# Pooled keys and values: one strided reduction in place of three additions

## Chip, core and metric

The kernel runs on one core of one Trainium2 chip. What is measured is the time of one execution in device microseconds (us). The engines of the core are named as in the profile: PE (TensorE matmuls), PEld (its weight loads), DVE (VectorE), ACT (ScalarE), POOL (GpSimd) and SP (SyncE, which issues most transfers).

## What is computed

Attention over keys and values that are averaged in groups of eight rows, then two feed-forward layers. Batch 8, 8 heads, 576 rows, head size 64; 4608 tokens of width 512, inner width 2048; float32.

```python
def _attn_ref(q, k, v):
    pool, Sp, scale = 8, S // 8, 1.0 / np.sqrt(D)
    k_p = k.reshape(B, H, Sp, pool, D).mean(axis=3)
    v_p = v.reshape(B, H, Sp, pool, D).mean(axis=3)
    scores = scale * np.matmul(q, k_p.transpose(0, 1, 3, 2))
    scores = scores - np.max(scores, axis=-1, keepdims=True)
    attn = np.exp(scores)
    attn = attn / (np.sum(attn, axis=-1, keepdims=True) + 1e-09)
    return np.matmul(attn, v_p)

x = attn_out.transpose(0, 2, 1, 3).reshape(B * S, H * D)
h = x @ moe_w_in;  x = np.maximum(0.01 * h, h) @ moe_w_out
h = x @ moe2_w_in; r = np.maximum(h, 0.0); out = (r * r) @ moe2_w_out
```

## The kernel before

Attention goes batch by batch (8), each in chunks of at most 128 query rows (five per batch). For each batch the pooled keys and values are prepared first. A head has 72 pooled rows: 64 of them lie in large tiles of 128 partitions (two heads, one above the other; two such pairs per tile), the last 8 of all heads together in one small tile of 64 partitions. The transfers of `load_main` (L354) and `load_rest` (L368) put the eight rows that belong together side by side in one partition, 8 x 64 = 512 words, so a large tile is 128 x 2 x 512 and a small one 64 x 1 x 512.

`pooled` (L340) sums the eight rows on DVE. It halves the width three times: 512 to 256 to 128 to 64 words per pooled row. The first two steps write into the tile itself, the last into the destination; each step reads what the one before wrote. For a large tile the steps are 512, 256 and 128 columns wide, for a small one 256, 128 and 64. The factor 1/8 is applied later by ACT.

`prepare_k` (L398) calls `pooled` for the small tile and for two large ones, then PE transposes the sums (L412, L415) and ACT writes the key matrix `kT`. `prepare_v` (L431) does the same for values: POOL multiplies the small sum by a mask (L437), transfers copy the product (L445), ACT and DVE split the large sums into a high and a low part (L459, L460). A batch thus has six sums, and there are eight batches.

Beside attention the first layer starts at once, on the tokens that are ready. Its weights are decoded on ACT and DVE (`decode`, L181: passes over 128 x 1024 words at L187 to L198, then L208; the inputs `low` and `high` take every second word of the staged tile) and split into two parts on ACT and DVE (L226, L227, and L807, L808 for the inner activations), because each product is made by three matmuls (L301). The staged weights come through a ring of two tiles.

The first batch is in an order written out by hand (`first_batch`, L621, held by `in_order`, L89: on each engine the instructions keep the order of the program). Behind it a planner orders the instructions of every engine, on the whole along the program's order, where steps of attention are dealt out between the units of the first layer (`advance`, L1077; rates at L60). Attention is done some 490 us into the span; later come the preparation of the second layer's weights and the block products of both layers.

Of the kernel before, what the change touches and what calls it, by code (L numbers as in the profile page):

```python
# [12 lines left out]
ALU = mybir.AluOpType  # L13
AX = mybir.AxisListType
# [4 lines left out]
POOL = 8  # L19
# [14 lines left out]
def attention_two_mlps(  # L34
# [11 lines left out]
    nc = tc.nc  # L46
    B, H, S, D = q.shape
# [261 lines left out]
    def attention():  # L309

        with ExitStack() as s:
# [10 lines left out]
                out=mask, in_=mask, compare_op=ALU.is_ge, fill=0.0, base=0,  # L322
# [3 lines left out]
                out=mask, in_=mask, compare_op=ALU.is_ge, fill=0.0, base=KR - 1,  # L326
# [12 lines left out]

            def pooled(dst, src):  # L340

                for n in (POOL * D // 2, POOL * D // 4, D):
                    nc.vector.tensor_tensor(
                        out=dst if n == D else src[:, :, 0:n], in0=src[:, :, 0:n], in1=src[:, :, n:2 * n], op=ALU.add
                    )

            def kv_tile(b, rows, n, name):

# [49 lines left out]
            def prepare_k(b):  # L398
                kr, kk = KV.pop(("k", b))
                i = b % 2  # L400
                kd = ap1.tile([P, NP, D], F32, tag="kd", name=f"kd{b}")
                rr = ap1.tile([KR * H, 2, D], F32, tag="rr", name=f"rr{b}")
                pooled(rr[:, 0:1], kr)
                nc.vector.tensor_copy(rr[:, 1], rr[:, 0])
                for m in range(0, NP, 2):
                    pooled(kd[:, m:m + 2], kk[m // 2])
                    yield
# [23 lines left out]
            def prepare_v(b):  # L431
                vr, vv = KV.pop(("v", b))
                vd = ap1.tile([P, NP, D], F32, tag="vd", name=f"vd{b}")
                rd = ap1.tile([KR * H, 1, D], F32, tag="rd", name=f"rd{b}")
                pooled(rd, vr)
                rv = ap1.tile([KR * H, H, D], F32, tag="rv", name=f"rv{b}")
                nc.gpsimd.tensor_tensor(  # L437
# [35 lines left out]
            for b in range(B):  # L473
                at = 0
                for span in range(len(SPANS)):
                    off = 0
                    while off < SPANS[span]:
                        n = min(P, SPANS[span] - off)
# [704 lines left out]
```

## Time and profile before

| | us |
|---|---|
| median of 3 runs | 1657.63 (1656.99 to 1659.5) |
| profiled run | 1661.4 |
| span of the profiled execution | 1659.6 |
| DVE busy in the span | 1277.1 (77%) |
| PE busy in the span | 1609.5 (97%) |
| POOL busy in the span | 130.2 (8%) |
| L343 busy on DVE, 0 to 400 us | 69.3 |

The profile is one execution; the span is from its first to its last instruction, and the run's time holds 1.8 us more. Busy shares over the whole span mix stages with different limits, so they are read stretch by stretch. The chain of work that ended last is followed back from the last instruction.

### The profile page before, as it was taken

The numbers are of one execution on the slowest core, as the hardware profiler recorded it, in microseconds if no ns is written. First come the engines' busy times: TensorE is split into PE (matmuls) and PEld (weight loads), VectorE is DVE, ScalarE is ACT, GpSimd is POOL, SyncE is SP. The second block draws the span as 40 slices with busy tenths as digits, with TensorE's granted clock in tenths as the row PEclk, the third lists the DMA queues.
The fourth block names the chain that finished last, engine by engine and source line by source line (L and its number), as shares of the span: only waits on it lengthen the run. The fifth ranks groups of instructions, "written<-read, shape, count | busy, mean of one in ns | idle before, by whom it ended". The sixth has DMA issues, their size and how long they took to land.

```text
span 1659.6 us, 27187 instructions
## 1 busy us (share of the span) xinstructions
PE 1609.5 (97%) x9976; PEld 1514.8 (91%) x9976; DVE 1277.1 (77%) x1893; ACT 895.5 (54%) x1602; POOL 130.2 (8%) x149
## 2 busy tenths in 40 slices
PE   5889999999999999999999999999999999999998
PEld 4667778888888999999999999999999999999998
DVE  5999899878678988979989569378477486485474
ACT  5768655655667867667677425334234234244233
POOL 3131323223210000000000000000000000000000
PEclk8999999999999999999999999999999999999999
DMA  7666565867435778888897777878878878878775
GB/s 180 174 206 186 163 176 161 246 194 206 127 101 198 263 272 280 270 301 277 281 317 251 254 261 270 301 255 289 288 252 296 283 251 302 273 253 272 265 251 190
DMA packets 223716, 399.74 MB, mean 241 GB/s; under 512 B 56160, under 2 KB 129888, under 8 KB 223584
## 3 DMA queue, kind: packets, MB, share of 16 engines
q1 hardware_dynamic: 223264, 397.48, 72.6%
q8 instruction: 80, 1.31, 0.3%
q10 hardware_dynamic: 320, 0.52, 0.1%
q14 instruction: 52, 0.43, 0.1%
HBM read 318.77 MB, written 77.59 MB: 239 GB/s over the span
## 4 chain that ended last, share of the span: by engine, by line
PE 81%; DVE 10%; DMA 3%; ACT 3%; issue 2%; SPq 0%; POOL 0%; ACTq 0%; DVEq 0%; POOLq 0%
PE h L304 13%; PE h L306 13%; PE h L305 13%; PE acc L306 12%; PE acc L304 12%; PE acc L305 12%; PE s L513 1%; DVE gl L808 1%; DVE wm L198 1%; ACT x L530 1%; DMA wb_in<-ws_in 1%; PE pt L563 1%; DMA st_in_out<-in_moe_w_out_dram 1%; PE trq L492 1%; DVE ol L868 1%
## 5 line engine op out<-in xcount | busy, mean ns | idle before, releaser
L867 ACT CAST oh<-g 128x768 fp32r<-128x768 f32 x252 | 210.2, 835 | 261.9 <-PE acc L305 163.6
L304 PE MATMUL h<-xh,wb_in 128*128 128x384 f32 x1008 | 338.0, 335 | 5.5 <-ACT s L970 3.9
L306 PE MATMUL h<-xh,wb_in 128*128 128x384 f32 x1008 | 337.5, 335 | 0.0
L305 PE MATMUL h<-xl,wb_in 128*128 128x384 f32 x1008 | 337.4, 335 | 0.0
L868 DVE TENSOR_TENSOR ol<-g,oh 128x768 fp32r<-128x768 f32 x252 | 240.3, 953 | 81.2 <-ACT oh L867 80.8
L306 PE MATMUL acc<-wb_out,ol 128*128 128x256 f32 x1008 | 282.2, 280 | 0.0
L304 PE MATMUL acc<-wb_out,oh 128*128 128x256 f32 x1008 | 281.2, 279 | 0.0
L305 PE MATMUL acc<-wb_out,oh 128*128 128x256 f32 x1008 | 281.2, 279 | 0.0
L304 PEld LDWEIGHTS h<-xh,wb_in 128*128 128x128 f32 x1008 | 189.8, 188 | 7.4 <-ACT s L970 4.5
L306 PEld LDWEIGHTS h<-xh,wb_in 128*128 128x128 f32 x1008 | 189.7, 188 | 0.0
L305 PEld LDWEIGHTS h<-xl,wb_in 128*128 128x128 f32 x1008 | 189.7, 188 | 0.0
L305 PEld LDWEIGHTS acc<-wb_out,oh 128*128 128x128 f32 x1008 | 189.5, 188 | 0.0
L306 PEld LDWEIGHTS acc<-wb_out,ol 128*128 128x128 f32 x1008 | 189.2, 188 | 0.0
L304 PEld LDWEIGHTS acc<-wb_out,oh 128*128 128x128 f32 x1008 | 188.5, 187 | 0.0
L871 DVE TENSOR_TENSOR g<-g,g 128x768 f32<-128x768 f32 x144 | 135.8, 952 | 1.1
L304 PE MATMUL h<-xh,hl_in 128*128 128x512 f32 (+1 forms) x320 | 124.1, 388 | 11.4 <-ACT hl_in L226 6.0
L976 DVE TENSOR_TENSOR g<-h,s 128x768 f32<-128x768 f32 x36 | 34.4, 956 | 125.6 <-issue 75.2
L304 PE MATMUL acc<-gh,hl_out 128*128 128x512 f32 (+1 forms) x320 | 120.0, 383 | 1.2 <-ACT hl_out L226 1.1
L306 PE MATMUL h<-xh,hl_in 128*128 128x512 f32 (+1 forms) x320 | 120.8, 377 | 0.1
L305 PE MATMUL h<-xl,hl_in 128*128 128x512 f32 (+1 forms) x320 | 120.3, 376 | 0.0
L944 DVE SCALAR_TENSOR_TENSOR g<-g 128x768 f32<-128x768 f32 x96 | 91.2, 954 | 37.3 <-ACT g L993 36.4
L305 PE MATMUL acc<-gl,hl_out 128*128 128x512 f32 (+1 forms) x320 | 118.5, 373 | 0.9 <-DVE gl L808 0.9
(149 smaller groups left out, 3138.0 us busy)
## 6 DMA issues: line engine op xcount, KB each, us to landing
wb_in<-wd_in SPq DMA_DIRECT2D x204, 512.0 KB, 4.2
wb_out<-wd_out SPq DMA_DIRECT2D x204, 512.0 KB, 4.4
xs<-x SPq DMA_DIRECT2D x18, 768.0 KB, 6.2
wb_in<-ws_in SPq DMA_DIRECT2D x48, 256.0 KB, 4.3
wb_out<-ws_out SPq DMA_DIRECT2D x48, 256.0 KB, 3.3
out_dram<-o SPq DMA_DIRECT2D x24, 384.0 KB, 5.1
q<-in_q_dram SPq DMA_DIRECT2D x32, 256.0 KB, 3.8
v<-in_v_dram SPq DMA_DIRECT2D x64, 128.0 KB, 3.7
```

The lines of the kernel that those rows point to most:

```text
L198: nc.vector.scalar_tensor_tensor(out=m, in0=high, scalar=0xC0000000, in1=m, op0=ALU.bitwise_and, op1=ALU.bitwise_or)
L304: nc.tensor.matmul(outp, ah, bh, start=first, stop=False, **kw)
L305: nc.tensor.matmul(outp, ah, bl, start=False, stop=False, **kw)
L306: nc.tensor.matmul(outp, al, bh, start=False, stop=last, **kw)
L492: nc.tensor.transpose(tr[:, m, :n], t[:n, 2 * m:2 * m + 2].rearrange("p a d -> p (a d)"), ident[:n, :n])
L513: nc.tensor.matmul(sc[:n, 2 * m:2 * m + 2].rearrange("p a x -> p (a x)"), qT[:, 2 * e + m, :n], kT[b % 2][:, 2 * e + m].rearrange("p a x - ...
L530: nc.scalar.activation(x[:n, 4 * e + h], sc[:n, h], AF.Exp, bias=mx[:n, h], accum_out=sm[:n, 4 * e + h],)
L867: nc.scalar.copy(hi, src)
L868: nc.vector.tensor_tensor(out=lo, in0=src, in1=raw(hi), op=ALU.subtract)
L871: nc.vector.tensor_tensor(out=out_, in0=a, in1=b, op=ALU.subtract)
L944: nc.vector.scalar_tensor_tensor(out=g, in0=g, scalar=0.0, in1=g, op0=ALU.max, op1=ALU.mult)
L976: nc.vector.tensor_tensor(out=g11, in0=v, in1=s1, op=ALU.add)
```

## The change

Only `pooled` changes. The three additions become one reduction. Its input is a view of the same tile in which, for each pooled row m and each column d, the eight values j stand innermost; since a row of 64 words lies between two of them, neighbouring elements of the view are 64 words apart. The tile is no longer written. Every call, its place in the program and its destination stay.

```diff
             def pooled(dst, src):
 
-                for n in (POOL * D // 2, POOL * D // 4, D):
-                    nc.vector.tensor_tensor(
-                        out=dst if n == D else src[:, :, 0:n], in0=src[:, :, 0:n], in1=src[:, :, n:2 * n], op=ALU.add
-                    )
+                nc.vector.tensor_reduce(
+                    out=dst, in_=src.rearrange("p m (j d) -> p m d j", j=POOL), axis=AX.X, op=ALU.add
+                )
```

## Rows read from the trace of the kernel before

**Rows 1.** The page: the chain that ended last, shares of the span by engine.
```profile
PE 81%; DVE 10%; DMA 3%; ACT 3%; issue 2%; SPq 0%; POOL 0%; ACTq 0%; DVEq 0%; POOLq 0%
```

**Rows 2.** By stretch: us; PE, PEld, DVE, ACT, POOL busy (instructions); clock; DMA share, GB/s.
```profile
0.00:40.00 40.00, 21.96 (x104) 18.40 (x105) 23.56 (x56) 23.29 (x106) 16.48 (x30) 0.89 0.75 182
40.00:200.00 160.00, 141.91 (x663) 110.85 (x662) 148.90 (x261) 117.58 (x315) 40.53 (x32) 0.95 0.62 183
200.00:320.00 120.00, 116.99 (x622) 96.76 (x621) 109.53 (x239) 69.70 (x160) 29.90 (x34) 1.00 0.63 187
320.00:400.00 80.00, 80.00 (x438) 67.45 (x437) 65.12 (x133) 44.08 (x93) 21.62 (x25) 1.00 0.71 206
```

**Rows 3.** The same stretches, line L343 alone: us, busy (instructions), clock, DMA.
```profile
0.00:40.00 40.00, 7.37 (x18) 0.89 0.75 182
40.00:200.00 160.00, 24.06 (x54) 0.95 0.62 183
200.00:320.00 120.00, 22.80 (x45) 1.00 0.63 187
320.00:400.00 80.00, 15.05 (x27) 1.00 0.71 206
400.00:1659.60 1259.60, 0.00 (x0) 1.00 0.75 257
```

**Rows 4.** DVE in order of time, 56 to 67 us: start, duration, instruction.
```profile
57.39 0.69 DVE L343 TENSOR_TENSOR k<-k 128x512 f32<-128x512 f32 x1
...
60.41 1.22 DVE L198 SCALAR_TENSOR_TENSOR wm<-st_in_out,wm 128x1024 uint32<-128x1024 uint32 x1
61.55 0.68 DVE L227 TENSOR_TENSOR hl_out<-w,hl_out 128x512 fp32r<-128x512 f32 x1
...
64.42 0.42 DVE L343 TENSOR_TENSOR k<-k 128x256 f32<-128x256 f32 x1
64.76 0.68 DVE L227 TENSOR_TENSOR hl_in<-w,hl_in 128x512 fp32r<-128x512 f32 x1
65.36 0.69 DVE L191 TENSOR_SCALAR wm<-wm 128x1024 f32<-128x1024 f32 x1
...
65.96 0.29 DVE L343 TENSOR_TENSOR kd<-k 128x128 f32<-128x128 f32 x1
66.16 0.69 DVE L194 TENSOR_SCALAR wm<-wm 128x1024 uint32<-128x1024 uint32 x1
```

**Rows 5.** DVE's groups by form: count | busy us, mean ns | idle before.
```profile
L343 DVE TENSOR_TENSOR v<-v 128x512 f32<-128x512 f32 x16 | 14.1, 880 | 0.9 <-DMA v<-in_v_dram 0.9
L343 DVE TENSOR_TENSOR vd<-v 128x128 f32<-128x128 f32 x16 | 9.0, 571 | 0.1
```

**Rows 6.** POOL and DVE in order of time at 82 us.
```profile
82.03 1.74 POOL L437 TENSOR_TENSOR rv<-rd,mask 64x512 f32<-64x512 f32 x1
...
82.54 1.38 DVE L343 TENSOR_TENSOR vd<-v 128x128 f32<-128x128 f32 x1
```

**Rows 7.** DVE's reductions and L198 by form; POOL's product in order of time.
```profile
L523 DVE TENSOR_REDUCE mx<-s 128x4 f32<-128x288 f32 x64 | 27.5, 453 | 7.7 <-PE s L513 6.9
L198 DVE SCALAR_TENSOR_TENSOR wm<-st_in_out,wm 128x1024 uint32<-128x1024 uint32 x16 | 19.6, 1226 | 0.1
L540 DVE TENSOR_REDUCE sm<-x 128x8 f32<-128x576 f32 x20 | 15.0, 749 | 3.2 <-ACT x L539 3.1
...
18.68 1.04 POOL L545 TENSOR_TENSOR p<-x,rs 128x512 f32<-128x512 f32 x1 [3.39 <-DVE rs L543]
```

**Rows 8.** All engines in order of time, first batch, 7 to 29 us.
```profile
7.84 1.15 DVE L343 TENSOR_TENSOR k<-k 128x512 f32<-128x512 f32 x2 [1.76 <-DMA k<-in_k_dram]
...
10.76 0.47 PE L412 MATMUL trk<-ident,kd 128*128 128x128 f32 x1 [0.85 <-DVE kd L343]
...
26.23 1.15 DVE L343 TENSOR_TENSOR v<-v 128x512 f32<-128x512 f32 x2
...
28.18 1.04 POOL L545 TENSOR_TENSOR p<-x,rs 64x512 f32<-64x512 f32 x1 [5.52 <-ACT qT L496]
```

## The prediction, made before the result

> **What bounds the kernel now.** I read the page first: TensorE (PE) carries 81% of the chain that ended last, VectorE (DVE) 10% of it [rows 1]. A whole-span average hides the stage, so I then cut the span into stretches [rows 2]. From 400 us on, the changed code is gone: line L343 has no instruction there [rows 3], and from 320 us to 400 us PE has no idle time at all. What is changed can only act before 320 us. In 0 to 40 us PE is busy 22.0 of 40 us: this is the hand-ordered first batch. In 40 to 200 us PE is busy 141.9 of 160 us, so it loses 18.1 us, and DVE is busy 148.9 us, so DVE has only 11.1 us left: there DVE is the tightest engine. In 200 to 320 us PE loses 3.0 us of 120. After 320 us PE is full, so the change is worth what it does to PE's start on that full stretch: at most PE's idle time ahead of it can be won, and any time by which DVE delays PE there is lost for good.
>
> **What the change removes.** Six sums are made per batch (for keys and for values: one of 64 partitions, two of 128), eight batches, 48 sums. Each is three additions now, 144 instructions, and becomes one reduction, 48. The trees occupy DVE 7.4 us in 0 to 40 us (18 instructions, four large and two small sums), 24.1 us in 40 to 200 us (54: twelve large, six small), 22.8 us in 200 to 320 us (45: ten large, five small) [rows 3]. The 15.1 us after 320 us lie beside a full PE and are priced at nothing; without that cover they would count as those of the stretch before.
>
> How long a tree really holds DVE is seen in the start times, since neighbours overlap: behind an addition of 512 columns the next instruction starts 0.60 us later, behind 256 columns 0.34, behind 128 columns 0.20 us, and behind a pass over 1024 columns 1.14 us [rows 4]. So a large tree that is not disturbed costs 0.60 + 0.34 + 0.20 = 1.14 us, although its three durations add to 1.4 us: the removal of two instructions is worth far less than their durations. The tree reads 896 pairs, the reduction reads 1024 single elements; the tree pays three starts, the reduction one. At equal speed per element they draw.
>
> What the trees do lose is time beside GpSimd (POOL): the rows of values stand at a mean of 880 ns for 512 columns and 571 ns for 128 [rows 5], against 0.69 and 0.29 us where POOL is idle [rows 4]. One case: an addition of 128 columns takes 1.38 us while POOL's product with the mask takes 1.74 us [rows 6]. That is why 24.1 us stand in 40 to 200 us where twelve large sums at 1.14 us and six small ones at about 0.67 (0.34 + 0.20 + some 0.13 us for 64 columns, an estimate) would make 17.7. A reduction reads one tensor, so this loss may go; it may also just pass to the additions of other lines that are then beside POOL. The Trainium skill, "SBUF — State Buffer", section "Who interferes with whom", says that a reduction never contends with GpSimd while an addition of two SBUF tensors does; the stretched rows agree with the second half, no row shows the first, and by it all of the loss of L343 goes (some 6 us in 40 to 200 us).
>
> **What it adds: a read that steps 64 words.** The view puts the eight rows innermost, so each next element lies 256 bytes on. No row shows such a read. Lower end: DVE's reductions take 453 ns for 288 elements and 749 ns for 576, thus 1.03 ns an element, and 1024 elements give 749 + 448 x 1.03 = 1210 ns; the pass of L198, of which one input is every second word, takes 1226 ns for 1024 [rows 7]. So at full speed a large sum holds DVE 1.14 us and a small one (512 elements) 0.60. Upper end: the slowest read of 4-byte elements from SBUF that the trace has is POOL's, 1.04 us for 512, 2.03 ns an element [rows 7]; it is another engine, hence only an end. At that speed a large sum takes 1024 x 2.03 = 2.08 us plus 0.08 us of spacing (1.14 less 1024 x 1.04), 2.16 us, a small one 1.12 us. I take the upper end: every full-speed row of DVE reads all words or every second one, this reads one in 64, which is far outside of what these rows cover. Both ends stay for the range. I know no reason by which the read could be faster than the lower end.
>
> The Trainium skill speaks against the change too: "Vector Engine (DVE) Microarchitecture Reference", section "5.2 Measured stream behaviour on trn2 (trn3 not measured)", has a port at full rate only where runs of two adjacent words are read, else 1.73 ns a column for one hopping source and up to 2.50 for small steps. L198 contradicts it at a step of two words, where full speed is measured [rows 7]; at 64 words nothing here can tell. By 1.73 ns the sum below would be about +5 us, by 2.50 about +18.
>
> **The sum**, upper end.
> - 0 to 40 us. The order is fixed there. The two key sums stand one behind the other on the path: the first starts at 7.84 us, and PE's transpose that waits for the second starts at 10.76 us [rows 8]. With reductions it starts near 7.84 + 2 x 2.16 + 0.15 = 12.3 us, +1.6. The second value sum at 26.23 us stands ahead of the instructions that release POOL at 28.18 us [rows 8]: 2.2 for 1.5 us, +0.7; the first (16.02 us) I count at +0.2, since DVE waits for ACT soon after. The small sums wait for their DMA and cost nothing. Sum +2.5 us.
> - 40 to 200 us. 12 x 2.16 + 6 x 1.12 = 32.6 us against 24.1: +8.5 us of DVE work, and some +1.5 if part of POOL's contention passes to neighbours: +10. DVE's 11.1 us idle can swallow some; I let 0.6 of it reach PE (ends: 0 and 1): +6 us.
> - 200 to 320 us. 10 x 2.16 + 5 x 1.12 = 27.2 against 22.8: +4.4 us. PE loses 3.0 us in 120 here and is nearly covered: a quarter, +1 us.
>
> Together +9.5 us. The profiled run is 1661.4 us (span 1659.6 and 1.8 us around it), which becomes 1670.9; it is 0.2% above the median of 1657.6, so the timed kernel should come at 1657.6 + 9.5 = **1667 us**.
>
> **Rivals.**
> 1. *The strided read is at full speed.* For it: the reduction rows and L198 [rows 7]. Against: none of them steps as far. 0 to 40 us: the transpose starts at 7.84 + 1.14 + 1.27 = 10.25 for 10.76 us, and 0.3 us more at the value sums, -0.8. 40 to 200 us: 12 x 1.14 + 6 x 0.60 = 17.3 for 24.1 us, -6.8, less 1.5 that passes to neighbours, times 0.6: -3.2. 200 to 320 us: 10 x 1.14 + 5 x 0.60 = 14.4 for 22.8, -8.4, a quarter: -2. Sum -6 us: 1652 us, faster. It decides from the speed at which the stretch of 40 to 200 us draws: 24.1 us = 12 x (1024 x + 0.08) + 6 x (512 x + 0.08) gives x = 1.48 ns an element; below that, faster.
> 2. *The stride costs, and slack takes it.* A tree's steps are spread out: the first addition of a key tile starts at 57.39 us, the last ends only after 65.96 us, other work between them [rows 4]. One instruction may deliver the sum sooner even if it is longer, and DVE's 11.1 us idle take the rest: about 1658 us, no change.
> 3. *Dearer than the upper end.* At a quarter above POOL's row, 2.54 ns (an estimate), a large sum holds DVE 2.68 us and a small one 1.38, and what is queued behind it on DVE, the splits that the first layer's matmuls wait for, comes late by that. 40 to 200 us: 12 x 2.68 + 6 x 1.38 = 40.4, +16.3 and 1.5, times 0.6: +10.7; 0 to 40 us +4.1, counted as above; 200 to 320 us 33.7, +10.9, a third, as DVE fills: +3.6. Sum +18 us, 1676. PE's granted clock, on average 0.89 in 0 to 40 us and 0.95 in 40 to 200 us [rows 2], part 2.4 and part 1.2 GHz, would have room to fall where PE waits more: each hundredth over these 200 us is some 2 us more.
>
> In all of them the planned order outside the first batch may shift, as two of three steps vanish; the nearest row is PE's idle time in 200 to 320 us, 3 us, which I take as the size of it, either way.
>
> **How the numbers follow.** Forecast 50%, full speed 27%, slack 13%, dearer 10%. A measurement of this kernel tells about 0.2%, 3.3 us. Of the forecast's 50%, 42 are slower, 6 the same, 2 faster; of full speed 17 faster, 9 the same, 1 slower; of slack 7 the same, 3 and 3; dearer is slower throughout. Faster 0.22, same 0.22, slower 0.56. The forecast's own range is 1660 to 1674 us. The range for 8 in 10 takes in the full-speed case's sum less 2 us, 1650, and reaches into the dear one at 1678.
>
> **What would show it.** The duration of a 128-partition reduction decides: 1.2 us is rival 1, 2.2 us the forecast, above 2.5 us rival 3. In the chain, the key transposes at 10.8 us should move to about 12.3 us; the stretch 40 to 200 us should end later with PE idle time up by some 6 us and DVE still above 90%; from 320 us on both kernels should run alike. I am wrong if reductions beside POOL are stretched as the additions were, if the order of the planned part changes by more than 3 us, or if PE's idle time does not follow DVE's load.

## The result, and the profile after

The changed kernel takes 1683.7 us (median of 4 runs, 1679.96 to 1685.67) against 1658.57 us of the kernel before (median of 4): ratio 1.0145, 95% interval [1.0129, 1.0161]. It is 24 us slower. The forecast was slower too, but 1667 us, with 1678 us as the top of the range: the sign held, the size did not.

The page of the changed kernel, its chain that ended last by engine, looks almost as that of [rows 1]. A percent of the span is 17 us, so these shares cannot show where 24 us go.

```profile
PE 80%; DVE 10%; DMA 4%; ACT 2%; issue 2%; SPq 1%; POOL 1%; DVEq 0%; ACTq 0%; POOLq 0%
```

The stretches of [rows 2], with the same columns (us; PE, PEld, DVE, ACT, POOL busy with instructions; clock; DMA):

```profile
0.00:40.00 40.00, 22.20 (x101) 19.16 (x102) 25.11 (x43) 23.19 (x105) 15.98 (x28) 0.83 0.67 175
40.00:200.00 160.00, 136.55 (x616) 107.22 (x614) 151.61 (x209) 109.82 (x285) 34.46 (x29) 0.91 0.62 178
200.00:320.00 120.00, 112.74 (x575) 92.52 (x573) 106.08 (x197) 64.14 (x162) 26.29 (x34) 0.95 0.58 170
320.00:400.00 80.00, 77.75 (x413) 64.52 (x414) 63.01 (x111) 44.72 (x96) 16.91 (x23) 1.00 0.66 198
```

The number to follow is the count of PE instructions, the progress of the work. By 40 us the changed kernel is 3 behind, by 200 us 50 (717 against 767), by 320 us 97, by 400 us 122. Before, PE does some 5.5 a us in 320 to 400 us (438 in 80), so the 122 are some 22 us. Stretch by stretch 3, 47, 47 and 25 instructions are missing; at the rate of the kernel before in each (2.6, 4.1, 5.2 and 5.5 a us) these are some 1, 11, 9 and 5 us, where the forecast had 2.5, 6, 1 and 0. The loss begins at 40 us and still grows after 320 us. The granted clock, a mix of 2.4 and 1.2 GHz in the means below 1, is lower in three of the stretches: 0.83 for 0.89, 0.91 for 0.95, 0.95 for 1.00.

PE's idle time in 40 to 200 us is up by 5.4 us (160 less 136.55, against 160 less 141.91), close to the 6 us that the forecast named as its sign. But idle time is only half of the loss. Busy time in the whole span, before and after:

```profile
PE 1609.5 (97%) x9976; PEld 1514.8 (91%) x9976; DVE 1277.1 (77%) x1893; ACT 895.5 (54%) x1602; POOL 130.2 (8%) x149
```

```profile
PE 1620.8 (96%) x9976; PEld 1523.3 (91%) x9976; DVE 1297.3 (77%) x1797; ACT 893.4 (53%) x1602; POOL 121.9 (7%) x149
```

The same 9976 PE instructions are busy 11.3 us longer, while the span of the profiled execution grows by 21.7 us (1659.6 to 1681.3). The lower granted clock stands beside it in three of the stretches; how much of the 11.3 us it makes is not shown.

L343 alone, now L342, answers [rows 3] (us, busy, clock, DMA):

```profile
0.00:40.00 40.00, 9.52 (x6) 0.83 0.67 175
40.00:200.00 160.00, 30.46 (x18) 0.91 0.62 178
200.00:320.00 120.00, 20.12 (x12) 0.95 0.58 170
320.00:400.00 80.00, 15.13 (x9) 1.00 0.66 198
400.00:1681.30 1281.30, 5.08 (x3) 1.00 0.78 256
```

The sums hold DVE 80.3 us in place of 69.3, 11 us more. The whole of DVE, by the two pages above, is busy 20.2 us longer (1297.3 for 1277.1), so its other instructions take 9 us more too. The kernel loses 24. DVE's groups by form (count, busy us, mean ns, idle before) give the price of the strided read, which no row of before had:

```profile
L342 DVE TENSOR_REDUCE vd<-v 128x128 f32<-128x1024 f32 x16 | 32.0, 2012 | 0.2
L342 DVE TENSOR_REDUCE kd<-k 128x128 f32<-128x1024 f32 x16 | 31.7, 1991 | 4.0 <-PE trk L411 2.5 <-DMA k<-in_k_dram 1.6
L342 DVE TENSOR_REDUCE rr<-rk 64x64 f32<-64x512 f32 x8 | 8.5, 1065 | 5.1 <-DMA rk<-in_k_dram 5.1
L342 DVE TENSOR_REDUCE rd<-rv 64x64 f32<-64x512 f32 x8 | 8.5, 1057 | 1.3 <-DMA rv<-in_v_dram 1.3
```

From the two sizes: (2002 - 1061) / 512 = 1.84 ns an element, below the 2.03 that the forecast took. The value sums, which stood beside POOL, are no slower than the key sums: the stretch of [rows 5] is gone.

In the first batch (all engines in order of time) the step goes the way that was forecast, at about half the size: the key transpose of [rows 8] starts at 11.59 us for 10.76 (forecast 12.3), POOL's product at 29.22 for 28.18.

```profile
7.87 3.66 DVE L342 TENSOR_REDUCE kd<-k 128x128 f32<-128x1024 f32 x2 [1.57 <-DMA k<-in_k_dram]
...
11.59 0.48 PE L411 MATMUL trk<-ident,kd 128*128 128x128 f32 x1 [1.25 <-DVE kd L342]
...
26.82 1.92 DVE L342 TENSOR_REDUCE vd<-v 128x128 f32<-128x1024 f32 x1
...
29.22 1.03 POOL L544 TENSOR_TENSOR p<-x,rs 64x512 f32<-64x512 f32 x1 [4.85 <-ACT vM L458]
```

So the reductions are cheaper than priced and the kernel is slower than forecast. That leaves two suspects: the planner's order outside the first batch, which did change (on DVE other instructions than the sums stand elsewhere in it, from the 68th place on), or the worth that the forecast gave to DVE's time.

### The profile page after: what moved, and what is told of

It is laid out like the page before. It is cut to its first block, busy times and chain, and to the rows that moved or that the text cites. A ratio compares the mean times of both kernels' runs of the same rounds, so it can differ in the third digit from the quotient of the medians.

```text
span 1681.3 us, 27104 instructions
## 1 busy us (share of the span) xinstructions
PE 1620.8 (96%) x9976; PEld 1523.3 (91%) x9976; DVE 1297.3 (77%) x1797; ACT 893.4 (53%) x1602; POOL 121.9 (7%) x149
## 4 chain that ended last, share of the span: by engine, by line
PE 80%; DVE 10%; DMA 4%; ACT 2%; issue 2%; SPq 1%; POOL 1%; DVEq 0%; ACTq 0%; POOLq 0%
PE acc L305 13%; PE acc L304 13%; PE acc L306 13%; PE h L304 13%; PE h L306 13%; PE h L305 13%; PE s L512 1%; DMA k<-in_k_dram 1%; DVE kd L342 1%; DVE gl L807 1%; PE trq L491 1%; DVE wm L198 1%; DVE mx L522 1%; DMA wb_in<-ws_in 1%; PE pt L562 1%
```

## Experiment 1: order or duration

Two orders, three ways to sum. Where an order is held, every engine's instructions are chained in that order by dependencies without a wait, from a list that is read out of the other kernel's program; an order that lists three additions puts a reduction at the place of the last, and the other way round three additions at the place of one reduction. The dense read adds eight neighbouring words instead of the eight rows, so it shows the price of the stride and is no replacement. The chain, and the dense read:

```diff
+    for order in FIXED_ORDERS:          # one per engine, by instruction name
+        for ins, last in zip(order[1:], order):
+            tc.add_manual_dep(ins, last.name, DependencyInfo(NoSync, DATA), reason="fixed")
```

```diff
-                    out=dst, in_=src.rearrange("p m (j d) -> p m d j", j=POOL), axis=AX.X, op=ALU.add
+                    out=dst, in_=src.rearrange("p m (d j) -> p m d j", j=POOL), axis=AX.X, op=ALU.add
```

**The strided reduction in the old order.**

> The strided reduction as changed, but on every engine the instructions stand in the order that the kernel before has (each reduction at the place of the last of its three additions). Theory A, the duration of the reductions (2.0 us for a large one, 80 us of DVE in all against 69) makes the loss: 1680 to 1685 us, as with the change. Theory B, the planner's other order makes most of it: only the 11 us of added DVE work stay, at 0.6 some 7 us, 1663 to 1668 us.

Measured: ratio 1.0166 [1.0143, 1.0188], 1687.0 us. The loss stays in full with the old order, as theory A had it (2 us above its range).

**The three additions in the new order.**

> The three additions as before, but on every engine in the order that the changed kernel has (the three stand together at the place of the reduction). Theory A: the order is worth little, 1655 to 1662 us. Theory B: the order carries most of the loss, 1672 to 1680 us.

Measured: 1.0077 [1.0047, 1.0108], 1669.5 us: between the two. The additions stand back to back in this order, each on the result of the one before, and no longer overlap: a large sum holds DVE for 1.40 us (58.34 to 59.74 in the lines below), where additions among other work take 1.14. That this makes the whole 13 us is not shown.

```profile
58.34 1.15 DVE L345 TENSOR_TENSOR k<-k 128x512 f32<-128x512 f32 x2
59.53 0.29 DVE L345 TENSOR_TENSOR kd<-k 128x128 f32<-128x128 f32 x1
59.74 0.69 DVE L193 TENSOR_SCALAR wm<-wm 128x1024 f32<-128x1024 f32 x1
```

**The dense reduction in the new order.**

> The changed kernel in its own order, but the reduction reads eight neighbouring words in place of eight words that lie 64 apart, so the sums are those of wrong elements; all else is equal. Theory A (duration): a large reduction takes 1.2 us and the time falls below that of the kernel before, 1651 to 1657 us. Theory B (order): the order stays, so 1670 to 1678 us.

Measured: 1.0002 [0.9990, 1.0015], 1659.8 us. The order of the changed kernel loses nothing when the read is dense. With reductions it is not the cause. But neither theory's number came: A had expected a gain.

**The dense reduction in the old order.**

> Reduction over eight neighbouring words (sums of wrong elements), on every engine in the order of the kernel before. Both theories: 1650 to 1657 us, since the reductions take 1.2 us and the order is the old one; what it lies under the kernel before is the worth of one dense reduction in place of three additions.

Measured: 1.0025 [1.0011, 1.0040], 1662.6 us: no gain either, and outside of what both had expected.

What one dense reduction in place of three additions is worth thus hangs on the order: it gains 12 us in the new one (1.0002 against 1.0077, with 5 us of noise) and loses 4 in the old one (1.0025). Why the old order does not suit it is not shown. The reduction stands there at the place of the last addition, takes 1.21 us for its 0.29, and so the sum is ready later; no run took this apart.

So the stride alone is worth 1.0145 against 1.0002, some 24 us, in either order (1.0166 against 1.0025). A dense reduction takes what the lower end said, and the value sums, some of which run beside POOL, are as fast as the key sums. The dense kernel's forms, and its stretches of 40 to 200 and 200 to 320 us:

```profile
L343 DVE TENSOR_REDUCE vd<-v 128x128 f32<-128x1024 f32 x16 | 19.2, 1211 | 0.2
L343 DVE TENSOR_REDUCE kd<-k 128x128 f32<-128x1024 f32 x16 | 19.2, 1208 | 4.7 <-PE trk L412 2.5 <-DMA k<-in_k_dram 2.2
L343 DVE TENSOR_REDUCE rr<-rk 64x64 f32<-64x512 f32 x8 | 5.4, 672 | 4.9 <-DMA rk<-in_k_dram 4.9
...
40.00:200.00 160.00, 142.52 (x667) 112.84 (x666) 147.85 (x227) 117.72 (x318) 32.84 (x32) 0.95 0.66 190
200.00:320.00 120.00, 114.66 (x602) 94.46 (x601) 103.68 (x205) 67.07 (x153) 27.10 (x34) 0.99 0.62 184
```

Per sum the stride adds 2.00 - 1.21 = 0.79 us (large) and 1.06 - 0.67 = 0.39 us (small): 32 x 0.79 + 16 x 0.39 = 31.5 us of DVE time. Of these 31.5 us, 24 reach the end.

## Experiment 2: where the loss falls

The changed kernel's order, with a strided read in some batches and a dense one in the others. Each difference from the dense run below carries some 3 us of noise either way, by the intervals of the two runs.

```diff
+                far = b == 0                 # 0 < b < 4;  b in (4, 5);  b > 5
+                view = "p m (j d) -> p m d j" if far else "p m (d j) -> p m d j"
```

> Order of the changed kernel; only the first batch's six reductions read words 64 apart, all others read neighbours (sums of wrong elements from the second batch on). Added DVE work against the all-dense run: 4 x 0.8 + 2 x 0.4 = 4 us. The forecast's step for 0 to 40 us put 3.3 us between full and low speed: 1662 to 1664 us. If the loss is dealt out over all batches alike (24 us over 8): 1663 us. If the path of the first batch takes nothing: 1660 us.

Measured: 1.0014 [1.0003, 1.0025], which is 0.0012 or 2 us above the dense run, not clear of the noise.

> Only the second to fourth batch (reductions at some 56 to 184 us) read words 64 apart; the others read neighbours (sums of wrong elements). Added DVE work 6 x 0.8 x 1 + 3 x 2 x 0.4 + 6 x 0.8 = 12 us. Forecast's step (0.6 of the added work reaches TensorE in 40 to 200 us): +7, 1667 us. If DVE is the bound there: +12, 1672 us. Alike over all batches: +9, 1669 us.

Measured: 1.0080 [1.0065, 1.0094], 13 us above the dense run. Within the noise, all of the 12 us of DVE time comes out at the end.

> Only the fifth and sixth batch (some 205 to 293 us) read words 64 apart; the others read neighbours (sums of wrong elements). Added DVE work 8 us. Forecast's step (a quarter reaches TensorE in 200 to 320 us): +2, 1662 us. Alike over all batches: +6, 1666 us. DVE is the bound: +8, 1668 us.

Measured: 1.0038 [1.0024, 1.0051], 6 us above: three quarters of the 8 us; a quarter, 2 us, lies outside of the noise.

> Only the last two batches (some 320 to 402 us) read words 64 apart; the others read neighbours (sums of wrong elements). Added DVE work 8 us. Forecast's step (TensorE is full there, priced at nothing): 1660 us. Alike over all batches: +6, 1666 us. If TensorE's cover there holds only while DVE is not behind from earlier batches, it stays at 1660 us here and the loss after 320 us in the changed kernel is a debt of the earlier batches.

Measured: 1.0034 [1.0022, 1.0045], 5 us above: two thirds, in a stretch that the forecast priced at nothing.

The four add to 26 us, the whole is 24: the batches pay each for themselves (for the first alone that is not clear of the noise), and the last two pay without any debt from earlier ones. The stretch of 320 to 400 us, dense first and then with the last two batches strided, shows how:

```profile
320.00:400.00 80.00, 80.00 (x435) 67.33 (x436) 59.98 (x114) 44.37 (x96) 18.79 (x25) 1.00 0.69 202
```

```profile
320.00:400.00 80.00, 78.70 (x421) 65.03 (x422) 63.74 (x109) 43.23 (x95) 17.46 (x24) 1.00 0.68 199
```

PE was "busy" 80.0 of 80 us and DVE 60, which read as cover. With DVE at 63.7 us PE is idle for 1.3 us and completes 421 instructions for 435. A PE that is busy all the time by the profile is not one that nothing can delay.

## Experiment 3: DVE's time, or a sum that comes late

A dense reduction, and behind it a second one that nobody uses, so that DVE is held as by the strided read while the sum is ready early; and the strided read in two instructions. Both in the changed kernel's order on every engine.

```diff
+                nc.vector.tensor_reduce(
+                    out=spare[:rows, :n], in_=src[:, :, 0:352 if n == 2 else 296], axis=AX.X, op=ALU.add
+                )
```

> Order of the changed kernel on every engine; each reduction reads neighbours (sums of wrong elements, 1.2 us) and is followed on DVE by a second reduction over 704 words (296 in a small tile) whose result nobody uses, 0.8 and 0.4 us: DVE is held as long as by the strided reduction, but the sum itself is ready early. If the loss is time taken from DVE: 1680 to 1686 us, as the change. If it is the sum that comes late to its readers: 1659 to 1664 us, as the dense reduction alone.

Measured: 1.0149 [1.0125, 1.0174], 1682.7 us, the same as the change. The second reduction takes 0.87 us, some 0.8 without the overlap with its neighbour, and 0.44 in small tiles:

```profile
L347 DVE TENSOR_REDUCE vd<-v 128x128 f32<-128x1024 f32 x16 | 19.4, 1211 | 0.2
L353 DVE TENSOR_REDUCE spare<-v 128x2 f32<-128x704 f32 x16 | 14.0, 874 | 0.0
L353 DVE TENSOR_REDUCE spare<-rv 64x1 f32<-64x296 f32 x8 | 3.5, 442 | 0.0
```

```diff
+                view = src.rearrange("p m (j d) -> p m d j", j=POOL)
+                for half in (slice(0, D // 2), slice(D // 2, D)):
+                    nc.vector.tensor_reduce(out=dst[:, :, half], in_=view[:, :, half], axis=AX.X, op=ALU.add)
```

> The changed kernel in its order, each strided reduction cut into two of half the columns, one behind the other: the same reads, no instruction over some 1.1 us. If the length of one instruction matters (what is queued behind it is held up): at most 1678 us. If only the sum of DVE's time counts: 1682 to 1688 us.

Measured: 1.0144 [1.0123, 1.0165], 1681.8 us. Neither the stride as such nor the length of one instruction is needed for the loss, nor that the sum is late: time taken from DVE at these places makes it.

## Experiment 4: why the dense reduction gains nothing

By its own rows it takes some 20 us less of DVE than the additions (its reductions are busy 49 us in all, the additions 69). The whole of DVE, though, is busy only 12 us less, 1265.5 for 1277.1:

```profile
PE 1608.9 (97%) x9976; PEld 1515.1 (91%) x9976; DVE 1265.5 (76%) x1797; ACT 894.5 (54%) x1602; POOL 115.7 (7%) x149
```

The other 8 us are back in other instructions of DVE; those of L248 (`s_out<-w`, eight of them), for one, go from 454 to 738 ns on average. That the stretch beside POOL passes to them, as the forecast allowed with 1.5 us, fits; it is not shown for all of the 8. So 12 us less yield nothing, while 31.5 us more cost 24. Three points on the same order, and one on the order of before, tell a knee from a straight line.

```diff
-                    out=dst, in_=src.rearrange("p m (j d) -> p m d j", j=POOL), axis=AX.X, op=ALU.add
+                    out=dst, in_=src[:, :, 0:256].rearrange("p m (d j) -> p m d j", j=4), axis=AX.X, op=ALU.add
```

> Order of the changed kernel; each reduction reads neighbours and only the first half of the words (four rows' worth, sums of wrong elements). DVE is held 32 x 0.53 + 16 x 0.26 = 21 us less than by the dense reduction. DVE's time worth the same on both sides (0.75): 1644 us. A knee at the dense level: 1657 to 1660 us.

> As the one before, a quarter of the words (sums of wrong elements): 32 us of DVE time less than the dense reduction. Worth the same on both sides: 1636 us. A knee: 1655 to 1660 us.

> Order of the changed kernel; dense reduction (sums of wrong elements) and behind it a second one over 288 words (104 in a small tile) that nobody uses: 32 x 0.38 + 16 x 0.19 = 15 us of DVE time more than the dense one. A straight line from 0 at the dense one to +23 at 33 us: 1669 us. If there is slack first and the full price only then: 1661 to 1664 us.

```diff
-                for n in (POOL * D // 2, POOL * D // 4, D):
+                for n in (POOL * D // 2, D):
```

> The kernel before in its own order on every engine, with the second of the three additions left out (the last then adds only a part of the rows): 32 x 0.34 + 16 x 0.20 = 14 us of DVE time less. DVE's time worth 0.75 of it: 1648 us. A knee at or near the level of before: 1655 to 1659 us.

Measured, with the runs above that share the order (us: ratio less 1, times the median of before):

| DVE time against the dense reduction | ratio | us against before |
|---|---|---|
| -32 us (a quarter of the words) | 0.9958 [0.9943, 0.9974] | -7 |
| -21 us (half of the words) | 0.9985 [0.9971, 0.9999] | -2.5 |
| 0 (dense) | 1.0002 [0.9990, 1.0015] | 0 |
| +15 us (half of the added read) | 1.0066 [1.0047, 1.0085] | +11 |
| +16 us (the three additions in this order; by DVE's busy time, 1281.4 for 1265.5) | 1.0077 [1.0047, 1.0108] | +13 |
| +32 us (whole added read) | 1.0149 [1.0125, 1.0174] | +25 |
| +31.5 us (strided, the change) | 1.0145 [1.0129, 1.0161] | +24 |
| two additions, old order: 14 us less than before (17.5 by busy time, 1259.6 for 1277.1) | 0.9967 [0.9955, 0.9980] | -5.5 |

Above the dense level a microsecond of DVE costs 0.7 to 0.8 us, and the three additions, which share this order too, lie on the same line. Below it a microsecond returns 7 / 32 = 0.2 on average, with 2 us of noise on each point; from the kernel before, 5.5 / 14 = 0.4, or 0.3 by busy time. It is a bend, not a wall: above, the straight line held (1670.4 us for 1669); below, the knee was nearer, and the times came out 1 to 3 us under its ranges. What DVE does with the time shows in its waits (who waits for what: us in total, times, longest) in 40 to 400 us, first before, then dense, then with a quarter of the words:

```profile
DVE gl L808 <- ACT gh L807: 4.3, 5, 2.5
DVE mx L523 <- PE s L513: 2.2, 5, 0.8
```

```profile
DVE gl L808 <- ACT gh L807: 12.0, 8, 4.3
DVE mx L523 <- PE s L513: 4.0, 6, 1.0
```

```profile
DVE gl L810 <- ACT gh L809: 13.3, 9, 4.3
DVE mx L525 <- PE s L515: 12.3, 11, 2.3
```

A DVE with less to do waits for ACT's high parts and for PE's scores, whose inputs come from DVE, ACT and PE in turn. That fits the bend; that these waits are its whole cause is not shown.

## Experiment 5: less DVE work by way of POOL

```diff
-                pooled(rr[:, 0:1], kr)
+                pooled(rr[:, 0:1], kr, nc.gpsimd if b else nc.vector)
-                pooled(rd, vr)
+                pooled(rd, vr, nc.gpsimd if b else nc.vector)
```

> The kernel before, with the three additions of the small tiles (from the second batch on, 14 sums) on POOL in place of DVE. It takes 14 x 0.67 = 9.4 us from DVE. If DVE's time is the bound as the runs so far say (0.75 us for each us): 1651 us. If POOL's additions hold up DVE's by as long as they run: 1658 us or more.

Measured: 1.0030 [1.0017, 1.0043], 1663.7 us: 5 us slower. POOL's first step takes 0.87 us for keys and 1.64 for values, against 0.41 to 0.43 us on DVE:

```profile
L343 POOL TENSOR_TENSOR rv<-rv 64x256 f32<-64x256 f32 x7 | 11.5, 1638 | 38.1 <-DMA rv<-in_v_dram 38.1
L343 POOL TENSOR_TENSOR rk<-rk 64x256 f32<-64x256 f32 x7 | 6.1, 871 | 35.9 <-DMA rk<-in_k_dram 35.9
```

Over the whole span DVE is busy 1277.7 us in place of 1277.1, so of the 9.4 us nothing is left, and POOL is held 13 us longer in 40 to 200 us (53.8 for 40.5). The order was not held in this run and changed too (on DVE other instructions than the sums stand elsewhere in it, from the 80th place on), so what POOL's part of the 5 us is stays open. No version here that adds the eight rows beats the kernel before.

## Experiment 6: which step costs

Behind the end of the changed kernel, reductions of 1024 words to 128 whose elements lie s words apart, in two turns; during the second, no other engine computes:

```diff
+        for s in (1, 2, 4, 8, 16, 32, 64, 128):
+            nc.vector.tensor_reduce(
+                out=to[:, 0, 0:128].rearrange("p (a s) -> p a s", s=s),
+                in_=flat.rearrange("p (a j s) -> p a s j", j=8, s=s), axis=AX.X, op=ALU.add)
```

> The changed kernel, and behind its end 16 reductions on DVE alone, of 1024 words to 128, with 1, 2, 4, 8, 16, 32, 64 and 128 words from one element to the next, twice, with additions between them. If every step off the neighbouring word costs: 1.2 us at 1, near 2.0 at 2 and above. If at least every second word is free, as L198 suggests: 1.2 us at 1 and 2, 1.9 to 2.0 from 4 on. If the cost grows with the step: rising from 4 to 128.

DVE in order of time (start, duration), the second turn, steps 1, 2, 4, 8, 16, 32, 64 and 128 from top to bottom; the first turn agrees within 0.1 us:

```profile
1683.18 1.21 DVE L1160 TENSOR_REDUCE step<-steps 128x128 f32<-128x1024 f32 x1
1684.30 1.21 DVE L1160 TENSOR_REDUCE step<-steps 128x128 f32<-128x1024 f32 x1
1685.43 1.95 DVE L1160 TENSOR_REDUCE step<-steps 128x128 f32<-128x1024 f32 x1
1687.30 1.97 DVE L1160 TENSOR_REDUCE step<-steps 128x128 f32<-128x1024 f32 x1
1689.19 1.85 DVE L1160 TENSOR_REDUCE step<-steps 128x128 f32<-128x1024 f32 x1
1690.95 1.86 DVE L1160 TENSOR_REDUCE step<-steps 128x128 f32<-128x1024 f32 x1
1692.73 1.86 DVE L1160 TENSOR_REDUCE step<-steps 128x128 f32<-128x1024 f32 x1
1694.51 1.86 DVE L1160 TENSOR_REDUCE step<-steps 128x128 f32<-128x1024 f32 x1
```

Steps 1 and 2 run at full speed, from 4 words on a large sum takes 1.85 to 1.97 us, whatever the step; the cost does not grow with it. In the kernel the step of 64 words takes 2.00 us, 0.14 us more than here; why is not shown.

## Why the prediction was right in sign and wrong in size

- **What bounds the kernel**: partly right. DVE is the tightest engine in 40 to 200 us, and there its added time comes out in full, within the noise. Wrong: "After 320 us PE is full", read as cover. Two strided batches there cost 5 us, and the last sums lie beyond 400 us by then.
- **The lower end and the draw**: right. A dense reduction takes 1.21 us as extrapolated [rows 7] and holds DVE 1.12 to 1.13 us by the start times of experiment 6, against 1.14 for three additions that nothing disturbs [rows 4]: they draw, as worked out. The draw of the two kernels (1.0002) is another matter, below.
- **The upper end**: right in choice, a little high in size: 2.00 us measured for a large sum, where the forecast counted 2.16 us for it. That it came so near is in part luck: the price was that of another engine's row, which was not even the slowest of the trace ([rows 6] has 1.74 us for 512 elements on POOL), and no run ties the two.
- **0 to 40 us**: right in mechanism; 2 us for the stride, with 3 us of noise, where the steps gave 3.3 between full and low speed.
- **The credit for time beside POOL**: wrong, and it is the first failed term. The stretched additions did vanish, as forecast for rival 1, but the forecast let the 24.1 us of the stretch, not the 17.7 of undisturbed additions, stand against the new reductions, and the gain is not there: rival 1 was to come at -6 us, and the dense runs measure 0 and +4. Of the 20 us that the sums' rows lose, 8 are back in other instructions of DVE, where the forecast counted 1.5; the other 12 bring no time. From this false start the sum of +9.5 us already lacked 6.
- **How much of DVE's time reaches PE**: wrong, and it is the larger term, most of all behind 200 us, where PE's small idle time was taken for cover. Taken as 0.6, a quarter and nothing for the three stretches after 40 us; measured, by batches that lie in them, 13 of 12 us, 6 of 8 and 5 of 8. The added work itself was nearly right on the whole of DVE: 20.2 us measured, and some 19 by the forecast's prices (3.5, 10 and 4.4 us in its three stretches and 1.3 behind them); it let 9.5 of them count, and 24 came. With the forecast's own way of counting from a dense draw at zero, 2 + 13 + 6 + 5 = 26 us.
- **PE's idle time as the measure of the loss**: right for the idle time (5.4 us more in 40 to 200 us, 6 forecast), wrong as the measure. PE's busy time for the same instructions was put at no change in the sum, and grew by 11.3 us.
- **Rival 3** gave 1676 us, and some 2 us more for each hundredth of granted clock: nearest to where the kernel landed, but by luck. It got there by a dearer read and by what is queued behind a long instruction; the read was not dearer, and halves of it lose as much. Its remark on the clock is borne out: the mean granted clock fell from 0.89 to 0.83 in 0 to 40 us and from 0.95 to 0.91 in 40 to 200 us, where PE finished less.
- **Rival 2**, a sum that is ready sooner and slack that takes the rest, is refuted by the run with the second, unused reduction: its sums are early, and it loses all the same.
- **The planner's order**, allowed for with 3 us either way: with reductions the two orders differ by 0.2%, as allowed; with additions in the new order it is 0.8%, more than allowed, so the order is no small thing for additions, though that case is not the change.
- **The range** failed by these two terms together: it reached to 1678 us only by a tenth of a chance on a dearer read, while a price near the taken one at full reach was not among the cases at all.

## What to carry to other kernels

Price an added load by the stretch in which the engine works, and take nothing as cover because another engine's busy share is 100%: count that engine's finished instructions, and let the price run up to the full added time. A saving and a cost on the same engine are not worth the same near the point where it becomes the bound: here 0.2 to 0.4 on one side and 0.7 to 1 on the other. And for a float32 reduction on DVE a strided view is free only while neighbours in the view lie within two words; one instruction in place of three is no gain where the three overlap at their ends, as among other work they do.

## What the runs showed of the hardware

- A reduction on DVE reads float32 at some 1.05 ns an element at a step of one word ((1.21 - 0.67) us over 512 elements) and takes as long at two; from four words on it is at some 1.7 to 1.8 ns (an estimate: 1.85 to 1.97 us less the 0.13 us that 1.21 us has beyond 1024 x 1.05 ns), the same at 16 and at 128. The Trainium skill, "SBUF — State Buffer", section "Specifications (TRN2)", gives lines of 16 bytes and wants two hits in each for full speed; the runs agree, since a step of two words makes two hits in four words and a step of four makes one. "Vector Engine (DVE) Microarchitecture Reference", section 5.2, asks for adjacent pairs of words; the step of two words, at 1.21 us, contradicts it, while its 1.73 ns for a hopping source is close to what 16 words and more show.
- Reductions beside POOL are not stretched (1211 ns for values and 1208 for keys, all 32 within 1.20 to 1.22 us; six of the value sums ran while POOL was at work), where additions of two tensors were (880 ns on average [rows 5], for 0.69 us at full speed [rows 4]). In the kernel with dense reductions POOL's own product is shorter too: here its groups before, then dense (busy us, mean ns).

```profile
L545 POOL TENSOR_TENSOR p<-x,rs 128x512 f32<-128x512 f32 (+1 forms) x40 | 58.7, 1468 | 302.3 <-DVE rs L543 156.6 <-DVE rd L343 36.9 <-PE h L306 21.3
```

```profile
L545 POOL TENSOR_TENSOR p<-x,rs 128x512 f32<-128x512 f32 (+1 forms) x40 | 47.8, 1195 | 241.2 <-DVE rs L543 201.4 <-ACT pt_h L564 16.8 <-PE pr L575 7.7
```

DVE is busy 12 us less in all (1265.5 for 1277.1) and POOL 15 us less (115.7 for 130.2), and the kernel is not faster for it. In the new order itself the dense reduction is 12 us faster than the additions, so what the freed time is worth cannot be read from one pair of kernels.
